# The order of a mixture-of-experts stage: small slots' weights behind the tile's, gates ahead of the routing's rest, tiles' experts behind the row list

## The chip, the cores and the metric

The kernel runs on one core of one Trainium2 chip. The metric is device time in microseconds (us) of one execution; three runs of the kernel before lie between 984.69 and 986.05 us, with a median of 985.2 us.

## The reference

Three stages in a row: attention with a memory term, a dense MLP on its output, and a mixture of experts (MoE), in which each of 2304 tokens goes to one of eight experts. The change touches the third stage alone.

```python
def _moe2_ref(x, w_gate, w_output_gate, w1, w2):
    logits = x @ w_gate
    e_idx = np.argmax(logits, axis=1)
    logits_s = logits - logits.max(-1, keepdims=True)
    probs = np.exp(logits_s)
    probs /= probs.sum(-1, keepdims=True) + 1e-09
    gate_w = probs[np.arange(N), e_idx]
    eom = 1.0 / (1.0 + np.exp(-(x @ w_output_gate)))
    for e in range(E):
        mask = e_idx == e
        h = np.maximum(x[mask] @ w1[e], 0.0)
        ye = h @ w2[e]
        out[mask] = gate_w[mask, None] * eom[mask, e, None] * ye
    return out

def reference(**kwargs):
    attn_out = _attn_ref(**attn_kwargs)
    x = np.ascontiguousarray(attn_out.transpose(0, 2, 1, 3)).reshape(B * S, H * D)
    x = _moe_ref(x=x, **moe_kwargs)
    return _moe2_ref(x=x, **moe2_kwargs)
```

N is 2304, D is 512, the hidden size F is 1024, and there are E = 8 experts. All data are float32.

## The kernel before

Attention and the MLP are interleaved and fill the first 700 us. The MLP's result is written to DRAM as `x2d`, one row per token, with four more columns for the gate factor. For the last block of tokens these columns are made late, by the generator `gates` (line 572): three small DVE operations, an Exp on ACT, three more DVE steps (line 578 on), and then the DMA of the rows to `x2d`.

The routing (`route`, line 820) counts tokens per expert and builds the order in which tokens are worked on. It is a generator; each `next(routing)` runs it to its next `yield`. It makes three lists. `idx` and `idxs` (line 914 on) name the token rows of each tile, from a one-hot product `inv` on TensorE (line 908) whose operand `rh` is made on DVE (lines 900 to 904). `ei` and `sw` (lines 901, 902) give each tile's expert, and whether it differs from that of the tile before; they come from the comparisons `c1` and `c2` (line 879 on). `idr`, `idq` and `esm` (lines 922 to 939) are rows and experts of the small slots, and need a second little product, `inq` (line 924), of `ivs` (line 922).

The experts' work is cut into tiles of 128 rows of one expert, numbered from 0. Tiles 0 and 1 belong to an expert picked early, from all but the last tokens; the routing's pieces are placed between their matmuls. The loop `tiles` (line 1078) does tiles 2 to 18, more if needed. In tile i, TensorE does the hidden layer (`hidden`, line 682: two halves of 512 columns, each in four steps of three matmuls, since each operand is split in a high and a low part), turns `hs`, the relu of the first half (`px`, line 667), and does the second layer (`result`, line 695, eight steps of three). Next to it ACT and DVE split the eight weight chunks of tile i+1, which lie in `st`, into `wH` (a cast, line 641) and `wL` (a subtraction, line 646); the same two engines split `hs` into `hH` and `hL` and the next rows into `xgH` and `xgL`. `Weights.fetch` (line 618) loads a chunk of 512 KB by a DMA from SP, under the condition that `sw` is not zero: a tile with the expert of the one before moves no data. A chunk's buffer comes free when its subtraction in the tile before is done.

Rows that do not fill a tile go into four small slots of 32 rows (`small`, line 1006), one beside each of the host tiles 4, 6, 9 and 11 (`HOSTS`). A slot's generator is started in the tile ahead of its host, where it reads its expert from `esm`, gathers its rows on POOL and loads its first four chunks (`sw`, line 1020). In the host it is moved on by `tick`, which `stepped` (line 1073) calls after each step of matmuls: turn of its rows and `xT`, product `ph` (line 1038) and the loads of its other four chunks (line 1022), relu `hq` (line 1043), turn `hT` (line 1049), nine empty steps, product `py` (line 1056), result `sy` (line 1060).

ACT, DVE, POOL and TensorE run the expert stage in the order in which the program is written. So do SP's DMAs, each behind the ones before it. The beginning of a tile reads, before the change:

```python
            if i + 1 in HOSTS and i + 1 < i1:
                ahead = small(HOSTS[i + 1])
                next(ahead)
            if i in HOSTS:
                beside = ahead
            more = i + 1 < i1
            w0, w = w, weights(i + 1) if more else None
            if i > i0:
                put(py, xlast, idxs[:, i - 1 : i])
            xnn = rows(idx[:, i + 2 : i + 3]) if i + 2 < i1 else None
            if more:
                w.fetch(0, 1, 2, 3, 4, 5, 7, 6)
```

Of the kernel before, what the change touches and what calls it, by code (L numbers as in the profile page):

```python
# [11 lines left out]
F32 = DT.float32  # L12
# [5 lines left out]
ALU = mybir.AluOpType  # L18
AX = mybir.AxisListType
# [3 lines left out]
P = 128  # L23
B, H, S, D = 4, 8, 576, 64
NT, DM, DFF = B * S, H * D, 2048
E, FF = 8, 1024
# [4 lines left out]
NS, SQ, SB = 4, 32, 4  # L31
NI = 24

NR = 19
HOSTS = {4: 0, 6: 1, 9: 2, 11: 3}
# [47 lines left out]
def tile_kernel(ctx, tc, qT, kT, qn, vx, z, beta, w_in, w_out, w_gates, w1, w2, out):  # L83
    nc = tc.nc
    PE, DVE, ACT, POOL, SP = nc.tensor, nc.vector, nc.scalar, nc.gpsimd, nc.sync
# [153 lines left out]
    c1 = at.enter_context(tc.tile_pool(name="c1", bufs=1, side="left"))  # L239
# [274 lines left out]
    part1, got = [], {}  # L514
# [98 lines left out]
    class Weights:  # L613
# [24 lines left out]
        def high(self, *cs):  # L638
            for c in cs:
                self.H[c] = self.pool.tile([P, 1024], F32R, name=f"wH{c}")  # L640
                ACT.copy(self.H[c], stage[c])  # L641
# [100 lines left out]
    def mid(x, n):  # L742

        return x.rearrange("p (o e) -> p o e", o=1).to_broadcast([P, n, x.shape[1]])

    def flat(x):
        return x.rearrange("p a b -> p (a b)")
# [72 lines left out]
    def route():  # L820
# [15 lines left out]
        DVE.tensor_copy(tt, tot)  # L836
        DVE.tensor_tensor(gtc, cnt.to_broadcast([P, E, NJ]), mid(io18, E), op=ALU.is_gt)
        yield
        DVE.tensor_tensor_scan(flat(inc), onef, flat(tt), 0.0, op0=ALU.mult, op1=ALU.add)
# [36 lines left out]
        DVE.tensor_copy(cf, ci)  # L876

        c1, c2 = (r2.tile([P, NI, E], F32, name=x) for x in ("c1", "c2"))
        DVE.tensor_tensor(c1, mid(flat(base), NI), itl.to_broadcast([P, NI, E]), op=ALU.is_le)
        DVE.tensor_copy(tf, ti)  # L880
        DVE.tensor_tensor(c2, mid(flat(end), NI), itl.to_broadcast([P, NI, E]), op=ALU.is_le)
        gates = got["gates"]
        next(gates)
        yield
        DVE.tensor_tensor(ohc[:, 0:6], mid(io128, 6), cf[:, 0:6].to_broadcast([P, 6, P]), op=ALU.is_equal)
        next(gates)
        DVE.tensor_tensor(c1, c1, c2, op=ALU.subtract)
        next(gates)
        DVE.tensor_tensor(ohc[:, 6:12], mid(io128, 6), cf[:, 6:12].to_broadcast([P, 6, P]), op=ALU.is_equal)
        next(gates)  # L890
        DVE.tensor_tensor(c1, c1, mid(io8, NI), op=ALU.mult)
        next(gates)
        yield
        DVE.tensor_tensor(ohc[:, 12:], mid(io128, NJ - 12), cf[:, 12:].to_broadcast([P, NJ - 12, P]), op=ALU.is_equal)
        yield
        ef = r2.tile([P, NI + 1, 1], F32, name="ef")
        DVE.memset(ef[:, 0:1], 0.0)
        DVE.tensor_reduce(ef[:, 1 : NI + 1], c1, axis=AX.X, op=ALU.add)
        rh = r2.tile([P, NJ, 3, NI + NS], BF16, name="rh")
        DVE.tensor_tensor(rh[:, :, 0], mid(ion, NJ), tf.to_broadcast([P, NJ, NI + NS]), op=ALU.is_equal)  # L900
        DVE.tensor_copy(ei, flat(ef)[:, 1 : NI + 1])
        DVE.tensor_tensor(sw, flat(ef)[:, 1 : NI + 1], flat(ef)[:, 0:NI], op=ALU.not_equal)
        DVE.tensor_scalar(rh[:, :, 1], rh[:, :, 0], iop, None, op0=ALU.mult)
# [10 lines left out]
        DVE.tensor_copy(idx, tok)  # L914

        DVE.tensor_scalar(iv[:, 0], iv[:, 0], -1.0e6, 1.0e6, op0=ALU.mult, op1=ALU.add)
        DVE.tensor_tensor(tok, tok, iv[:, 0], op=ALU.add)
# [3 lines left out]
        ivs = r.tile([P, 3, NS], BF16, name="ivs")  # L921
        DVE.tensor_copy(ivs, inv3[:, :, NI:])
        inq = ps_g.tile([P, 512], F32, name="inq", tag="pg")[:, : 3 * NS]
        PE.matmul(inq, lhsT=four, rhs=ivs.rearrange("p a n -> p (a n)"), start=True, stop=True)
# [8 lines left out]
        DVE.tensor_copy(idq, tks)  # L933
        c3 = r.tile([P, NS, E], F32, name="c3")
        DVE.tensor_tensor(c3, mid(flat(key), NS), ion[:, 1 : NS + 1].rearrange("p (n o) -> p n o", o=1).to_broadcast([P, NS, E]), op=ALU.is_equal)
        DVE.tensor_tensor(c3, c3, mid(io8, NS), op=ALU.mult)
        ef3 = r.tile([P, NS, 1], F32, name="ef3")
        DVE.tensor_reduce(ef3, c3, axis=AX.X, op=ALU.add)
        DVE.tensor_copy(esm, flat(ef3))
        yield  # L940
# [48 lines left out]
    def hidden_out():  # L989
        return hp_.tile([P, FF], F32, name="hs"), [hp_.tile([P, 8, P], F32R, name=f"h{x}") for x in "HL"]  # L990
# [15 lines left out]
    def small(s):  # L1006
# [32 lines left out]
        while len(ws) < 2 * KD:  # L1039
            fetch()  # L1040
        yield
        hq = smp.tile([P, FF // 4], F32, name="hq")
        ACT.activation(hq, ph, AF.Relu)
# [5 lines left out]
        ACT.copy(hT, pt.rearrange("p (c t) -> p c t", c=2))  # L1049
        for _ in range(9):  # L1050
            yield
# [19 lines left out]
    def stepped(g, n):  # L1071

        for _ in range(n):
            r_ = next(g)
            tick()
        return r_

    def tiles(i0, i1, w, xg, xn, xx):
        nonlocal beside, smp
        for i in range(i0, i1):  # L1080
            if i + 1 in HOSTS and i + 1 < i1:
                ahead = small(HOSTS[i + 1])
                next(ahead)
            if i in HOSTS:
# [6 lines left out]
            if more:  # L1091
                w.fetch(0, 1, 2, 3, 4, 5, 7, 6)
            high, low = (w.high, w.low) if more else (lambda *cs: None,) * 2

            hs, hh = hidden_out()
            tick()
# [10 lines left out]
            DVE.tensor_tensor(hh[1][:, 0:4], px, f32(hh[0][:, 0:4]), op=ALU.subtract)  # L1107
            ph = stepped(g, 2)
            high(3)
            relu(hs, ph, 1)  # L1110
# [31 lines left out]
    routing = route()  # L1142
# [77 lines left out]
```

## Time and profile before

| | us |
|---|---|
| median of the three runs | 985.2 |
| profiled execution, its own time | 991.04 |
| span of the profiled execution | 989.2 |
| TensorE (PE) busy | 917.4, 93% of the span |
| VectorE (DVE) busy | 622.1 |
| ScalarE (ACT) busy | 520.3 |
| GpSimd (POOL) busy | 367.7 |
| mean granted clock of TensorE | 0.973 |

Engine times are busy times in the one profiled execution, and L667 is line 667 of the kernel. In a row of the time line stand the start in us from the span's start, the duration in us, the engine, the line, the operation, its output <- its inputs, the shapes and the number of instructions that the row merges; in brackets, the idle time of the engine just before and what ended it. A row of busy time by stretches has the stretch, its length, then the busy us (and instructions) of PE, PEld (loads of the stationary operand), DVE, ACT and POOL, the granted clock as a share of 2.4 GHz, the share of time in which the DMA engines were busy, and GB/s. A row of waits says which instruction waited for which, us in total, how often, and the longest. In the page's groups of instructions the mean in ns of one follows the busy time.

### The profile page before, as it was taken

How to read it: one execution, taken by the hardware profiler on the slowest of the kernel's cores; microseconds unless marked ns; L12 is line 12 of the kernel's file. 1: busy time of each engine (PE TensorE's matmuls, PEld its weight loads, DVE VectorE, ACT ScalarE, POOL GpSimd, SP SyncE). 2: the span in 40 equal slices, each digit the busy share in tenths (PEclk: the TensorE clock that was granted, in tenths of full speed). 3: DMA queues.
4: the chain of work that ended last, by engine and by line, in shares of the span. 5: the costliest groups of instructions: out<-in, count | busy, mean ns of one | idle time of the engine just before them, and what ended most of it. 6: DMA issues, size and time to landing. Idle time of an engine off the chain costs nothing. (4 is left out here: it accounts for less than half of the span.)

```text
span 989.2 us, 17067 instructions
## 1 busy us (share of the span) xinstructions
PE 917.4 (93%) x5733; PEld 720.5 (73%) x5733; DVE 622.1 (63%) x1511; ACT 520.3 (53%) x1084; POOL 367.7 (37%) x574
## 2 busy tenths in 40 slices
PE   4677799999999999899999999999887999999996
PEld 2344477777776777788888888888766778778875
DVE  6766797565657541778344444447767668678982
ACT  5556666565546543445222222223346668768883
POOL 1543376445546552435533333335221123112210
PEclk9987799999999999989999999999999999999998
DMA  6432332221213010543011111112323565532850
GB/s 196 129 100 95 118 117 71 76 75 54 75 54 100 14 35 17 176 129 128 22 44 44 43 44 43 45 43 107 107 76 118 204 240 190 204 130 104 319 201 23
DMA packets 49278, 101.70 MB, mean 103 GB/s; under 512 B 5341, under 2 KB 15581, under 8 KB 49184
## 3 DMA queue, kind: packets, MB, share of 16 engines
q1 hardware_dynamic: 45696, 89.74, 26.8%
q0 software_dynamic: 3488, 10.80, 3.2%
q8 instruction: 47, 0.77, 0.3%
q14 instruction: 47, 0.39, 0.1%
HBM read 136.66 MB, written 14.72 MB: 153 GB/s over the span
## 5 line engine op out<-in xcount | busy, mean ns | idle before, releaser
L646 DVE TENSOR_TENSOR wL<-st,wH 128x1024 fp32r<-128x1024 f32 x136 | 163.7, 1227 | 43.2 <-ACT wH L641 37.5
L213 PE MATMUL hps<-xH,wH 128*128 128x256 f32 x576 | 166.8, 290 | 1.6 <-ACT xH L91 1.4
L213 PE MATMUL hps<-xL,wH 128*128 128x256 f32 x576 | 162.2, 282 | 2.9 <-DVE xL L200 2.9
L95 POOL TENSOR_SCALAR gH<-g 128x256 fp32r<-128x256 f32 x144 | 63.6, 441 | 271.8 <-DVE g L217 214.4
L365 POOL TENSOR_SCALAR a<-a,rs,omg 128x320 f32<-128x320 f32 (+4 forms) x160 | 126.9, 805 | 97.1 <-DVE rs L360 72.5
L213 PE MATMUL hps<-xH,wL 128*128 128x256 f32 x576 | 161.2, 280 | 0.0
L217 DVE SCALAR_TENSOR_TENSOR g<-g,hps 128x256 f32<-128x256 f32 x144 | 60.0, 417 | 146.4 <-ACT g L216 146.4
L641 ACT CAST wH<-st 128x1024 fp32r<-128x1024 f32 x136 | 139.7, 1053 | 8.5 <-DMA st<-w 8.4
L216 ACT ACTIVATE g<-hps,half 128x256 f32<-128x256 f32 x144 | 68.0, 472 | 137.4 <-PE hps L213 112.3
L213 PEld LDWEIGHTS hps<-xH,wH 128*128 128x128 f32 x576 | 108.9, 189 | 18.6 <-issue 12.6
L221 POOL TENSOR_TENSOR gL<-g,gH 128x256 fp32r<-128x256 f32 x144 | 115.4, 802 | 11.8
L213 PEld LDWEIGHTS hps<-xL,wH 128*128 128x128 f32 x576 | 109.1, 189 | 8.6 <-DVE xL L200 3.8
L352 ACT ACTIVATE a<-st,mn 64x64 f32<-64x64 f32 (+4 forms) x160 | 88.4, 555 | 48.0 <-DVE mn L343 48.0
L376 PE MATMUL pa<-ident,a 128*128 128x128 f32 (+1 forms) x480 | 81.9, 302 | 32.1 <-POOL a L365 28.5
L213 PEld LDWEIGHTS hps<-xH,wL 128*128 128x128 f32 x576 | 109.1, 190 | 0.1
L376 PEld LDWEIGHTS pa<-ident,a 128*128 128x128 f32 (+1 forms) x480 | 59.0, 151 | 60.6 <-POOL a L365 33.8
L182 PE MATMUL acc<-wH,gH 128*128 128x512 f32 x288 | 95.5, 413 | 1.3 <-POOL gH L95 1.2
L182 PE MATMUL acc<-wH,gL 128*128 128x512 f32 x288 | 91.7, 400 | 2.3 <-POOL gL L221 2.3
L337 PE MATMUL pa<-kd,qd 64*128 64x64 f32 (+5 forms) x384 | 83.7, 488 | 10.3 <-DVE mn L343 5.4
L182 PE MATMUL acc<-wL,gH 128*128 128x512 f32 x288 | 91.0, 397 | 0.0
L343 DVE CUSTOM_DVE_ANT_0 st<-pa,mask 64x64 f32<-64x64 f32 (+4 forms) x160 | 52.9, 372 | 33.0 <-PE pa L337 33.0
L182 PEld LDWEIGHTS acc<-wH,gL 128*128 128x128 f32 x288 | 54.2, 190 | 16.2 <-POOL gL L221 3.5
(239 smaller groups left out, 1674.6 us busy)
## 6 DMA issues: line engine op xcount, KB each, us to landing
st<-w SPq DMA_DIRECT2D x136, 512.0 KB
sw<-w SPq DMA_DIRECT2D x32, 512.0 KB
w<-w_in SPq DMA_DIRECT2D x16, 512.0 KB
w<-w_out SPq DMA_DIRECT2D x16, 512.0 KB
qnt<-qn SPq DMA_DIRECT2D x16, 320.0 KB
vt<-vx SPq DMA_DIRECT2D x16, 320.0 KB
x2d<-row SPq DMA_DIRECT2D x18, 258.0 KB
qd<-qT SPq DMA_DIRECT2D x16, 288.0 KB
```

The lines of the kernel that those rows point to most:

```text
L95: POOL.tensor_scalar(out, x, 1.0, 1.0, op0=ALU.mult, op1=ALU.mult)
L182: PE.matmul(acc[t], lhsT=gg[:, t * P : (t + 1) * P], rhs=ww[:, 512:1024], start=m == 0 and first, stop=m == HM - 1 and last)
L213: PE.matmul(hps, lhsT=ww[:, kk * P : (kk + 1) * P], rhs=xx[:, kk], start=k == 0, stop=k == 3 * KD - 1)
L216: ACT.activation(g, hps, AF.Relu, bias=half, scale=1.0 / 6.0)
L217: DVE.scalar_tensor_tensor(g, g, 1.0, hps, op0=ALU.min, op1=ALU.mult)
L221: ENG[GL].tensor_tensor(gL, g, f32(gH), op=ALU.subtract)
L337: PE.matmul(pss[j][: QN[i], o : o + k1 - k0], lhsT=self.qd[r, QS[i] : QS[i] + QN[i]], rhs=self.kd[r, k0:k1], start=True, stop=True)
L352: ACT.activation(self.a[j][:m, o + D : o + D + n], self.st[j][i][:m, :n], AF.Exp, bias=self.mn[j][:m, i : i + 1], scale=-1.0, accum_out=se ...
L365: ENG[NORM[i]].tensor_scalar(av, av, r[:m, i], omg[:m, h : h + 1], op0=ALU.mult, op1=ALU.mult)
L376: PE.transpose(psa[:, off : off + QN[i]], self.a[j][: QN[i], QO[i] + c * P : QO[i] + (c + 1) * P], ident[: QN[i], : QN[i]])
L641: ACT.copy(self.H[c], stage[c])
L646: DVE.tensor_tensor(self.L[c], stage[c], f32(self.H[c]), op=ALU.subtract)
```

## The change

Four things are moved; no operation is added or left out.

1. In `route`, the first step of `gates` is run three segments earlier, right after `gtc`; the other four steps stay beside the one-hot `ohc`.
2. `c1`, `c2`, `ef`, `ei` and `sw` are computed after `idx`, no longer before `rh`.
3. `esm` is computed ahead of the product `inq`, with a `yield` between them, and both pieces run inside tile 2: one at its start, one after the hidden layer. Before, they ran after tile 2.
4. In `tiles`, a small slot is started behind the tile's own `put`, `rows` and `fetch`; in `small`, four empty steps stand before `hq`, and six in place of nine before `py`.

```diff
@@ route
         DVE.tensor_tensor(gtc, cnt.to_broadcast([P, E, NJ]), mid(io18, E), op=ALU.is_gt)
+        gates = got["gates"]
+        next(gates)
         yield
...
         DVE.tensor_copy(cf, ci)
-
-        c1, c2 = (r2.tile([P, NI, E], F32, name=x) for x in ("c1", "c2"))
-        DVE.tensor_tensor(c1, mid(flat(base), NI), itl.to_broadcast([P, NI, E]), op=ALU.is_le)
         DVE.tensor_copy(tf, ti)
-        DVE.tensor_tensor(c2, mid(flat(end), NI), itl.to_broadcast([P, NI, E]), op=ALU.is_le)
-        gates = got["gates"]
-        next(gates)
         yield
         DVE.tensor_tensor(ohc[:, 0:6], mid(io128, 6), cf[:, 0:6].to_broadcast([P, 6, P]), op=ALU.is_equal)
         next(gates)
-        DVE.tensor_tensor(c1, c1, c2, op=ALU.subtract)
         next(gates)
         DVE.tensor_tensor(ohc[:, 6:12], mid(io128, 6), cf[:, 6:12].to_broadcast([P, 6, P]), op=ALU.is_equal)
         next(gates)
-        DVE.tensor_tensor(c1, c1, mid(io8, NI), op=ALU.mult)
         next(gates)
         yield
...
-        ef = r2.tile([P, NI + 1, 1], F32, name="ef")
-        DVE.memset(ef[:, 0:1], 0.0)
-        DVE.tensor_reduce(ef[:, 1 : NI + 1], c1, axis=AX.X, op=ALU.add)
         rh = r2.tile([P, NJ, 3, NI + NS], BF16, name="rh")
         DVE.tensor_tensor(rh[:, :, 0], mid(ion, NJ), tf.to_broadcast([P, NJ, NI + NS]), op=ALU.is_equal)
-        DVE.tensor_copy(ei, flat(ef)[:, 1 : NI + 1])
-        DVE.tensor_tensor(sw, flat(ef)[:, 1 : NI + 1], flat(ef)[:, 0:NI], op=ALU.not_equal)
...
         DVE.tensor_copy(idx, tok)
+        c1, c2 = (r2.tile([P, NI, E], F32, name=x) for x in ("c1", "c2"))
...
+        DVE.tensor_copy(ei, flat(ef)[:, 1 : NI + 1])
+        DVE.tensor_tensor(sw, flat(ef)[:, 1 : NI + 1], flat(ef)[:, 0:NI], op=ALU.not_equal)
...
         DVE.tensor_copy(ivs, inv3[:, :, NI:])
+        c3 = r.tile([P, NS, E], F32, name="c3")
...
+        DVE.tensor_copy(esm, flat(ef3))
+        yield
         inq = ps_g.tile([P, 512], F32, name="inq", tag="pg")[:, : 3 * NS]
...
         DVE.tensor_copy(idq, tks)
-        c3 = r.tile([P, NS, E], F32, name="c3")
...
-        DVE.tensor_copy(esm, flat(ef3))
         yield
@@ small
         yield
+        for _ in range(4):
+            yield
         hq = smp.tile([P, FF // 4], F32, name="hq")
...
-        for _ in range(9):
+        for _ in range(6):
             yield
@@ tiles
-            if i + 1 in HOSTS and i + 1 < i1:
-                ahead = small(HOSTS[i + 1])
-                next(ahead)
             if i in HOSTS:
                 beside = ahead
...
                 w.fetch(0, 1, 2, 3, 4, 5, 7, 6)
+            if i + 1 in HOSTS and i + 1 < i1:
+                ahead = small(HOSTS[i + 1])
+                next(ahead)
             high, low = (w.high, w.low) if more else (lambda *cs: None,) * 2
+            if i == 2:
+                next(routing)
             hs, hh = hidden_out()
...
             ph = stepped(g, 2)
+            if i == 2:
+                next(routing)
             high(3)
```

On ACT, in the routing beside tile 0's second layer, the order was (`t` is the gate's Exp of the logits, `so` the gate step's own Exp, `hH` the cast of the turned `hs`, `ys` the result of tile 0):

```order
L564 ACTIVATE t_7987<-t_7986 128x16
L671 CAST hH<-px 128x512
L576 ACTIVATE so<-so 128x2
L707 ACTIVATE ys<-py,xg 128x512
L693 ACTIVATE hs<-ph 128x512
```

and it is now

```order
L564 ACTIVATE t_7987<-t_7986 128x16
L576 ACTIVATE so<-so 128x2
L671 CAST hH<-px 128x512
L707 ACTIVATE ys<-py,xg 128x512
L693 ACTIVATE hs<-ph 128x512
```

The Exp of `so` now stands ahead of the cast of `hH`.

On SP, in tile 3, the first small slot's loads (`sw`, L1020, with the read of `esm` before them) stood ahead of the tile's own (`st`, L636). The brackets name what each waits for:

```order
L1009 TENSOR_LOAD esm [waits DVE_49]
...
L1020 DMA sw<-w 128x1024 [waits DVE_49,PE_49,DMAHW0_49,Activation_49,Pool_49]
...
L1020 DMA sw<-w 128x1024 [waits DMAHW1_49]
...
L1020 DMA sw<-w 128x1024 [waits DMAHW2_49]
...
L1020 DMA sw<-w 128x1024 [waits DMAHW3_49]
...
L636 DMA st<-w 128x1024 [waits DMAHW4_49,Activation_49]
...
L636 DMA st<-w 128x1024 [waits DMAHW5_49,Activation_49]
```

They now stand behind the last of the tile's eight:

```order
L636 DMA st<-w 128x2x512 [waits DMAHW5_49,DVE_49]
...
L636 DMA st<-w 128x2x512 [waits DMAHW6_49,DVE_49]
...
L636 DMA st<-w 128x2x512 [waits DMAHW7_49,DVE_49]
...
L1010 TENSOR_LOAD esm [waits DVE_49]
...
L1021 DMA sw<-w 128x1024 [waits DMAHW0_49,PE_49,Pool_49]
...
L1021 DMA sw<-w 128x1024 [waits DMAHW1_49]
```

The tile's eight have moved in front of the read of `esm`, and each now waits for a subtraction on DVE (DVE_49).

On ACT, in tile 4, a host tile, the small slot's `hq` and `hT` stood ahead of the casts of the first two weight chunks and the relu of `hs`:

```order
L1033 COPY xT<-px 128x128
L1043 ACTIVATE hq<-ph 128x256
L1049 COPY hT<-pt 128x256
L641 CAST wH_8784<-st 128x1024
L641 CAST wH_8786<-st 128x1024
L693 ACTIVATE hs<-ph 128x512
L641 CAST wH_8793<-st 128x1024
L1105 CAST hH<-px 128x512
L641 CAST wH_8817<-st 128x1024
L693 ACTIVATE hs<-ph 128x512
```

They now stand behind that relu, one on each side of the cast of `hH`:

```order
L1034 COPY xT<-px 128x128
L641 CAST wH_8777<-st 128x1024
L641 CAST wH_8779<-st 128x1024
L693 ACTIVATE hs<-ph 128x512
L641 CAST wH_8786<-st 128x1024
L1046 ACTIVATE hq<-ph 128x256
L1110 CAST hH<-px 128x512
L1052 COPY hT<-pt 128x256
L641 CAST wH_8817<-st 128x1024
L693 ACTIVATE hs<-ph 128x512
```

Between the two relus of `hs` ACT has two more operations than before.

## Rows read from the trace of the kernel before

**Rows 1.** Busy time by stretches, tile 3 and tile 5.
```profile
748.90:767.20 18.30, 14.38 (x61) 11.19 (x60) 11.91 (x21) 10.41 (x13) 3.07 (x3) 0.91 0.45 159
786.00:798.70 12.70, 12.70 (x61) 9.95 (x60) 11.73 (x12) 11.32 (x15) 4.66 (x3) 1.00 0.39 144
```

**Rows 2.** TensorE's waits, 711 to 768 us.
```profile
PE px L667 <- ACT hs L693: 4.8, 2, 3.9
PE inv L908 <- DVE rh L904: 1.4, 1, 1.4
PE inq L924 <- DVE ivs L922: 1.3, 1, 1.3
```

**Rows 3.** TensorE's waits, 768 us to the end.
```profile
PE px L667 <- ACT hs L693: 3.0, 4, 0.8
PE py L701 <- DVE hL L1107: 1.1, 4, 0.3
```

**Rows 4.** Time line of TensorE in tile 3.
```profile
757.25 0.66 PE L667 MATMUL px<-ident,hs 128*128 128x128 f32 x4 [3.92 <-ACT hs L693]
...
758.34 0.63 PE L688 MATMUL ph<-wH,xgL 128*128 128x512 f32 x1
...
761.86 0.39 PE L701 MATMUL py<-wH,hL 128*128 128x512 f32 x1
```

**Rows 5.** Time line of ACT in tile 3.
```profile
754.71 1.99 ACT L641 CAST wH<-st 128x1024 fp32r<-128x1024 f32 x2 [6.42 <-DMA st<-w]
```

**Rows 6.** Time line of SP's DMA issues in tile 3.
```profile
752.04 2.13 SPq L1020 DMA_DIRECT2D sw<-w  x4
754.62 13.96 SPq L636 DMA_DIRECT2D st<-w  x16
```

**Rows 7.** Time line of DVE at the start of tile 3.
```profile
749.08 0.17 DVE L926 COPY iq<-inq 128x12 f32<-128x12 f32 x1 [0.26 <-PE inq L924]
...
750.22 0.17 DVE L933 CAST idq<-tks 128x4 uint32<-128x4 f32 x1
...
750.96 0.17 DVE L939 CAST esm<-ef 128x4 int32<-128x4 f32 x1
```

**Rows 8.** Time line of ACT in the routing.
```profile
711.61 0.59 ACT L671 CAST hH<-px 128x512 fp32r<-128x512 f32 x1 [1.07 <-PE px L667]
720.22 0.20 ACT L576 ACTIVATE so<-so 128x2 f32<-128x2 f32 x1 [8.02 <-DVE so L575]
```

**Rows 9.** Time line of DVE in the routing.
```profile
712.94 0.68 DVE L672 TENSOR_TENSOR hL<-px,hH 128x512 fp32r<-128x512 f32 x1
...
719.54 0.35 DVE L881 TENSOR_TENSOR c<-end,itl 128x192 f32<-128x192 f32 x1
719.81 0.17 DVE L573 TENSOR_TENSOR t<-oh,lg 128x16 f32<-128x16 f32 x1
...
720.10 0.95 DVE L885 TENSOR_TENSOR ohc<-io,cf 128x768 bf16<-128x768 f32 x1
...
725.48 0.68 DVE L904 TENSOR_TENSOR rh<-rh,io 128x504 bf16<-128x504 bf16 x1
```

**Rows 10.** Time line of TensorE in the routing.
```profile
713.52 0.40 PE L701 MATMUL py<-wH,hH 128*128 128x512 f32 x1
```

**Rows 11.** Time line of ACT in tile 4, a host tile.
```profile
767.95 0.26 ACT L1033 COPY xT<-px 128x128 f32<-128x128 f32 x1
771.28 0.39 ACT L1043 ACTIVATE hq<-ph 128x256 f32<-128x256 f32 x1 [3.08 <-PE ph L1038]
772.30 0.37 ACT L1049 COPY hT<-pt 128x256 f32<-128x256 f32 x1 [0.64 <-PE pt L1047]
```

**Rows 12.** Busy time by stretches, 724 to 732 us.
```profile
724.00:732.00 8.00, 6.34 (x37) 5.08 (x37) 3.89 (x15) 0.81 (x2) 2.04 (x2) 0.79 0.46 134
```

**Rows 13.** The page's groups of instructions: a weight subtraction on DVE.
```profile
L646 DVE TENSOR_TENSOR wL<-st,wH 128x1024 fp32r<-128x1024 f32 x136 | 163.7, 1227 | 43.2 <-ACT wH L641 37.5
```

**Rows 14.** Busy time by stretches, the small slot's first load.
```profile
752.00:762.40 10.40, 6.48 (x25) 4.93 (x24) 5.87 (x6) 6.40 (x8) 2.96 (x3) 0.84 0.79 278
```

More of the change, by code (lines that the diff above doesn't have):

```diff
@@ L914, in route @@
         DVE.tensor_copy(idx, tok)
+        c1, c2 = (r2.tile([P, NI, E], F32, name=x) for x in ("c1", "c2"))
+        DVE.tensor_tensor(c1, mid(flat(base), NI), itl.to_broadcast([P, NI, E]), op=ALU.is_le)
+        DVE.tensor_tensor(c2, mid(flat(end), NI), itl.to_broadcast([P, NI, E]), op=ALU.is_le)
+        DVE.tensor_tensor(c1, c1, c2, op=ALU.subtract)
+        DVE.tensor_tensor(c1, c1, mid(io8, NI), op=ALU.mult)
+        ef = r2.tile([P, NI + 1, 1], F32, name="ef")
+        DVE.memset(ef[:, 0:1], 0.0)
+        DVE.tensor_reduce(ef[:, 1 : NI + 1], c1, axis=AX.X, op=ALU.add)
+        DVE.tensor_copy(ei, flat(ef)[:, 1 : NI + 1])
+        DVE.tensor_tensor(sw, flat(ef)[:, 1 : NI + 1], flat(ef)[:, 0:NI], op=ALU.not_equal)
         DVE.tensor_scalar(iv[:, 0], iv[:, 0], -1.0e6, 1.0e6, op0=ALU.mult, op1=ALU.add)
@@ L922, in route @@
         DVE.tensor_copy(ivs, inv3[:, :, NI:])
+        c3 = r.tile([P, NS, E], F32, name="c3")
+        DVE.tensor_tensor(c3, mid(flat(key), NS), ion[:, 1 : NS + 1].rearrange("p (n o) -> p n o", o=1).to_broadcast([P, NS, E]), op=ALU.is_equal)
+        DVE.tensor_tensor(c3, c3, mid(io8, NS), op=ALU.mult)
+        ef3 = r.tile([P, NS, 1], F32, name="ef3")
+        DVE.tensor_reduce(ef3, c3, axis=AX.X, op=ALU.add)
+        DVE.tensor_copy(esm, flat(ef3))
+        yield
         inq = ps_g.tile([P, 512], F32, name="inq", tag="pg")[:, : 3 * NS]
@@ L933, in route @@
         DVE.tensor_copy(idq, tks)
-        c3 = r.tile([P, NS, E], F32, name="c3")
[L935 to L938, printed above, removed]
-        DVE.tensor_copy(esm, flat(ef3))
         yield
```

## Prediction

> **What bounds the kernel now.** I read the busy time by stretches first, then TensorE's waits, then the time lines of the engines around the waits that are left. An ordinary tile of the expert stage, tile 5, takes 12.70 us, all of them busy on TensorE; ACT is busy for 11.32 and DVE for 11.73 of them [rows 1]. So TensorE sets the time there, and the other two have 1.0 to 1.4 us to spare. Tile 3 does the same work in 18.30 us, with 14.38 us of TensorE and a granted clock of 0.91 [rows 1]. From the routing to the end of tile 3 TensorE waits in three places that the change touches: 4.8 us for hs in two waits (the longest 3.9), 1.4 us for rh, 1.3 us for ivs [rows 2]. Behind it, one wait of 0.8 for hs and one of 0.3 for hL come back in each of the four host tiles, 3.0 and 1.1 us in all [rows 3]. No more than some 13 us are to be had from these waits and the slow clock that follows them.
>
> The wait of 3.92 us in tile 3 ends with the relu of hs [rows 4]. That relu stands on ACT behind two casts of weights, which begin at 754.71 after 6.42 us of waiting for a DMA of st [rows 5]. Those DMAs begin only at 754.62, because SP first issues the four DMAs of small slot 0 (752.04), and these need esm, which DVE writes last of all, at 750.96 [rows 6, 7]. The casts begin 0.09 us after the first st is issued, so this DMA moved nothing: tile 4 has tile 3's expert. SP held up work that needed no data.
>
> **A. Routing.** The change sets three DVE operations and an Exp on ACT ahead of the split of px, and takes c1, c2 and their followers out from before the row list.
>
> The loss first. In the new order ACT has the Exp ahead of the cast hH, which before began at 711.61 [rows 8]. The three operations cost DVE 0.29 us (719.81 to 720.10 [rows 9]). They begin where hL stood, at 712.94, so the Exp begins near 713.35, the cast (0.59) ends near 714.05, and hL begins 1.15 us later than before. DVE is served in order, so the whole routing chain behind hL is late by 1.15. TensorE wants hH at 713.52 [rows 10]: it stands for about 0.6, and 0.3 more for hL.
>
> Then the gain. The three operations leave their old place (0.29). Five operations of c1's kind (0.27 each by c2's 719.54 to 719.81 [rows 9]) and two small casts (about 0.1 each) leave too: 1.8 in all. They had also filled gaps between dependent operations; three such gaps open again, 0.1 to 0.15 each, so 1.4 remain. rh, whose last operation begins at 725.48 [rows 9], is ready 1.4 - 1.15, some 0.3 us earlier. TensorE waits for rh anyway (1.4 [rows 2]), so its new wait for hH is paid from that wait. The 0.9 us for hs that is the second wait in the 4.8 [rows 2] goes as well: it came from the old place of the Exp, at 720.22 on ACT ahead of the relu [rows 8]; but it too only moves into the wait for rh. **A is 0.3 us**; bounds -0.9 (DVE wins nothing back) and +1.4 (the cast is not held up). ei and sw come some 4 us later; tile 3's weights are issued later by that, under the hidden layer of tile 2, at no cost as long as they need no data.
>
> **B. Tile 2.** The wait of 1.3 us for ivs [rows 2] goes, since ivs is made at the tile's start, where DVE waits for casts. In return the chain from iq to idq, 749.08 to 750.39, 1.3 us [rows 7], stands between two weight subtractions in mid tile and delays the second hL. DVE has 1.0 us free in a tile [rows 1], so I let 0.35 us reach TensorE, and 0.05 for the matmul. **B is 0.9**, between 0 (all of the chain shows) and 1.3.
>
> **C. Tile 3.** esm is written in tile 2; the st DMAs of tile 3 are ahead of the small slot's. The casts find their data, the relu is in time. Tile 3 becomes like tile 5: 18.3 - 12.7 = **5.6 us** [rows 1]. The check: 3.92 of waiting, and then matmuls that take 0.63 in place of the usual 0.39 or so, some eight at about 0.2 us more from start to start [rows 4]. Bounds 4.5 and 5.6.
>
> **D. Host tiles.** Before, ACT does xT, then waits 3.08 us for the small product before hq, and 0.64 more for the turn before hT; only then come the two casts and the first relu of hs [rows 11]. Now xT is followed by casts and relu at once. Of the 3.0 + 1.1 us [rows 3] all goes, unless it comes back later in the tile: hq (0.39), hT (0.37) and the wait for the turn (up to 0.64) [rows 11] now stand between the two relus of hs, 1.4 us against the 1.4 us that ACT has free [rows 1]. What is late next is the second relu. I leave 0.2 us in each tile: **D is 3.3 us**, between 0 and 4.1.
>
> The last move, small slots' first weights behind the tile's, with their gather behind the tile's scatter and gather on POOL, I cost at nothing: a whole tile of 12.7 us covers it. What it costs without that cover is the last rival.
>
> The sum is 0.3 + 0.9 + 5.6 + 3.3 = 10.1 us. The profiled execution, 991.04 us (its span 989.2), would come to 980.9. It lies 5.8 above the median of the runs, 985.2; taking the same sum from that gives **975.1 us**.
>
> **Rivals.**
> *The clock stays up too.* From 724 to 732 the granted clock was 0.79 [rows 12]: TensorE at the lower level for some 3.4 of 8 us, a loss of 1.7. If the shorter stops leave it high, 973.4 us. Against it: A only moves the stops, it hardly shortens them.
> *The host tiles' waits move, and do not go.* ACT has no time over in these tiles, so the second relu takes the first one's place: D is 0, 978.4 us.
> *The Exp holds the routing up.* A is -0.9 and B 0: 977.2 us. For it: the cast behind a DVE result, on an engine that serves in order; against it: the 1.8 us taken out.
> *The change does not do what it says in tile 3.* The st DMAs now wait for tile 2's subtractions, which the iq chain pushes back. If the casts still wait as long, C is 0: 980.7 us. Against it: st 0 comes free after the first subtraction, most of a tile earlier.
> *Gains are swallowed*, by several of these together: within 0.2%.
> *Slower: the small slots' operands come late.* Their first four DMAs are issued behind the tile's eight, which wait for the subtractions that end the tile before, two of them at 1.23 us [rows 13]: up to 2.5 us into the tile ahead of the host. The host's small product cannot begin before xT is done, at 768.21 in a tile that begins at 767.2 [rows 11, 1]: 12.7 - 2.5 + 1.0 = 11.2 us from issue to need. Last time it took 10.4 us, at 278 GB/s, 2.9 MB with the gathers of that time [rows 14]. So it holds by a narrow margin, with the first chunk due first. It turns to a loss where the load takes over 14 us in all four hosts; at 16 us, 975.1 + 4 x 4.8 = 994 us. The Trainium skill, "DMA: Bandwidth & Descriptors", section "Queues, rings and completion order", says that a DMA engine takes one issuer's descriptors in ring order; both kinds of weights come from SP. By that rule a tile's eight chunks with data (4.2 MB) ahead of the small slot's would double the load, at that rate to some 23 us, and every host would lose about 11 us. The trace speaks against that here: those 2.9 MB hold four small chunks (2.1 MB) and no others, though st DMAs were issued from 754.62 on [rows 14, 6].
>
> **How the numbers follow.** Forecast 0.55, clock 0.15, host waits 0.12, Exp 0.07, tile 3 unmended 0.03, swallowed 0.03, late operands 0.05. The range takes in forecast, clock, host waits and Exp, with the bounds of A to D: **971.5 to 979.0 us**. A difference of 0.2% (2 us) is about what a measurement of this kernel can tell from none. Faster than that: 0.92; within it 0.03; slower 0.05.
>
> **What would show it.** Right: in tile 3 no wait of TensorE for hs and a clock of 1.00; the wait for ivs gone; in the host tiles less than 0.3 us for hs and hL together; a new wait of about 0.6 us for hH next to 714 us, and rh ready at most half a microsecond earlier than before. Wrong: a wait of TensorE for the small slots' weights or rows at the start of tiles 4, 6, 9 and 11; a tile 3 above 13.5 us; host tiles as long as before; a second relu of hs that TensorE waits for by more than half a microsecond.

## The result and the profile after

The changed kernel takes 975.77 us (median of four runs, 974.74 to 978.34), the kernel before 985.62 on the same chip (four runs, 984.69 to 986.71): a ratio of 0.9903, with an interval of 0.9881 to 0.9926. It is 9.85 us faster; 10.1 were predicted. The profiled execution took 974.74 us with a span of 973.0, against 991.04 and 989.2.

Of the 16.2 us between the two spans, 3.69 lie ahead of the first product of the routing, `pf` (711.96 and 708.27 us), where both kernels run the same instructions, so these belong to the executions and not to the change. From there on, TensorE's waits in the changed kernel, from 705 us on (what waited for which, us in total, times, the longest):

```profile
PE py L701 <- DVE hL L672: 1.5, 2, 0.8
PE inv L897 <- DVE rh L893: 1.1, 1, 1.1
PE pf L760 <- DVE ohb L822: 0.4, 1, 0.4
PE py L701 <- ACT hH L671: 0.4, 1, 0.4
```

The 4.8 and 1.3 us of [rows 2] and the 3.0 and 1.1 us of [rows 3] are gone. All that is left lies in the routing; from 728 us to the end the profile lists no wait of TensorE. The busy time by stretches of the changed kernel, tile 3 and then tile 5 (the columns of [rows 1]):

```profile
743.56:756.24 12.68, 12.68 (x61) 9.94 (x59) 11.63 (x12) 11.10 (x14) 3.53 (x3) 1.00 0.61 230
773.69:786.37 12.68, 12.68 (x61) 9.94 (x60) 11.74 (x12) 11.30 (x15) 3.11 (x3) 1.00 0.68 232
```

Tile 3 is now as long as tile 5, without an idle moment and at the full clock, where it took 18.30 us at 0.91 [rows 1]. The time line of SP's DMA issues beside it:

```profile
727.50 17.68 SPq L636 DMA_DIRECT2D st<-w  x16
746.04 2.06 SPq L1021 DMA_DIRECT2D sw<-w  x4
```

SP has issued the tile's last `st` (by 745.18) before it comes to the four loads of the small slot. These have 11.4 us up to the small product at 757.49, which waits for none of them; 11.2 were worked out in the prediction. ACT in host tile 4:

```profile
756.94 0.26 ACT L1034 COPY xT<-px 128x128 f32<-128x128 f32 x1
757.08 2.01 ACT L641 CAST wH<-st 128x1024 fp32r<-128x1024 f32 x2
761.82 0.60 ACT L693 ACTIVATE hs<-ph 128x512 f32<-128x512 f32 x1 [2.72 <-PE ph L688]
762.31 1.04 ACT L641 CAST wH<-st 128x1024 fp32r<-128x1024 f32 x1
763.25 0.39 ACT L1046 ACTIVATE hq<-ph 128x256 f32<-128x256 f32 x1
763.59 0.59 ACT L1110 CAST hH<-px 128x512 fp32r<-128x512 f32 x1
764.49 0.37 ACT L1052 COPY hT<-pt 128x256 f32<-128x256 f32 x1 [0.32 <-PE pt L1050]
764.76 1.05 ACT L641 CAST wH<-st 128x1024 fp32r<-128x1024 f32 x1
765.72 0.60 ACT L693 ACTIVATE hs<-ph 128x512 f32<-128x512 f32 x1
```

In the 3.08 us in which ACT stood for the small product [rows 11] it now does the two casts, and the first relu waits only for its own product. The second relu (765.72, done at 766.32) is ready 0.06 us before TensorE turns it at 766.38. In the other three host tiles these are 0.06 or 0.07 us, in ordinary tiles some 0.7: the room between the two relus is used up, and one more operation there would show.

The routing is the one place with new waits. In the changed kernel ACT and DVE read there, DVE first:

```profile
709.45 0.17 DVE L575 TENSOR_REDUCE so<-t 128x2 f32<-128x16 f32 x1
710.36 0.69 DVE L672 TENSOR_TENSOR hL<-px,hH 128x512 fp32r<-128x512 f32 x1 [0.74 <-ACT hH L671]
...
721.67 0.68 DVE L893 TENSOR_TENSOR rh<-rh,io 128x504 bf16<-128x504 bf16 x1
...
723.86 0.35 DVE L906 TENSOR_TENSOR c<-base,itl 128x192 f32<-128x192 f32 x1
...
726.34 0.34 DVE L918 CAST idxs<-tok 128x24 uint32<-128x24 f32 x1
726.43 0.68 DVE L672 TENSOR_TENSOR hL<-px,hH 128x512 fp32r<-128x512 f32 x1
```

```profile
709.65 0.20 ACT L576 ACTIVATE so<-so 128x2 f32<-128x2 f32 x1 [2.81 <-DVE so L575]
709.76 0.57 ACT L671 CAST hH<-px 128x512 fp32r<-128x512 f32 x1
```

The cast `hH` waits for the Exp, DVE stands 0.74 us for the cast, and the whole chain follows late, as foreseen. What was not foreseen is the last line of DVE above: the chain from `c1` to `sw` now stands between the row list and the next `hL`. TensorE's time line has the waits there; the last is the one for that `hL`, while the 0.65 us ahead of `inv` go on into the wait for `rh`, which TensorE has anyway:

```profile
710.38 0.50 PE L701 MATMUL py<-wH,hH 128*128 128x512 f32 x1 [0.38 <-ACT hH L671]
720.83 0.50 PE L701 MATMUL py<-wH,hL 128*128 128x512 f32 x1 [0.65 <-DVE hL L672]
722.40 0.85 PE L897 MATMUL inv<-rh,ohc 128*128 128x84 bf16 x18 [1.07 <-DVE rh L893]
727.17 0.50 PE L701 MATMUL py<-wH,hL 128*128 128x512 f32 x1 [0.83 <-DVE hL L672]
```

### The profile page after: what moved, and what is told of

It is laid out like the page before. It is cut to its first block, busy times and chain, and to the rows that moved or that the text cites. A ratio compares the mean times of both kernels' runs of the same rounds, so it can differ in the third digit from the quotient of the medians.

```text
span 973.0 us, 17079 instructions
## 1 busy us (share of the span) xinstructions
PE 910.9 (94%) x5733; PEld 715.8 (74%) x5733; DVE 623.0 (64%) x1511; ACT 520.5 (53%) x1084; POOL 367.8 (38%) x574
## 5 line engine op out<-in xcount | busy, mean ns | idle before, releaser
L708 POOL DMA_INDIRECT out<-ys,idxs x17 | 18.8, 1107 | 132.4 <-ACT ys L707 84.1
```

## The experiments

Twelve runs were made, of ten more kernels, of the changed kernel once more (after2) and of one of the ten once more (v1b), each beside the kernel before on the same chip. "To list" is the time from the start of `pf` to the start of `inv`, "to tile 2" that from `inv` to the turn of the rows of tile 2, each in the profiled execution. The four of the first group change the kernel before; the others change the changed kernel.

| kernel | median | ratio to before, interval | to list | to tile 2 |
|---|---|---|---|---|
| before (profile above) | 985.62 | | 14.25 | 6.96 |
| changed | 975.77 | 0.9903, 0.9881 to 0.9926 | 14.13 | 6.51 |
| e_hq | 981.83 | 0.9941, 0.9919 to 0.9964 | 14.23 | 6.97 |
| e_order | 981.01 | 0.9942, 0.9919 to 0.9965 | 14.23 | 5.40 |
| e_esm | 979.63 | 0.9941, 0.9918 to 0.9965 | 14.22 | 5.40 |
| e_tiles | 980.36 | 0.9937, 0.9916 to 0.9958 | 14.21 | 5.41 |
| e_noroute | 975.72 | 0.9879, 0.9858 to 0.9900 | 14.24 | 5.40 |
| u_gates | 975.82 | 0.9881, 0.9852 to 0.9909 | 13.11 | 6.50 |
| u_experts | 977.44 | 0.9916, 0.9884 to 0.9948 | 16.14 | 6.98 |
| v1 | 977.58 | 0.9894, 0.9861 to 0.9926 | 13.21 | 6.97 |
| after2 | 976.79 | 0.9890, 0.9849 to 0.9931 | 14.12 | 6.50 |
| v1b | 972.96 | 0.9851, 0.9815 to 0.9887 | 13.22 | 5.41 |
| x_behind | 998.67 | 1.0106, 1.0075 to 1.0137 | 14.13 | 6.50 |
| x_ahead | 1010.79 | 1.0199, 1.0142 to 1.0256 | 14.11 | 6.96 |

### One part of the change alone, on the kernel before

**e_hq**: only the later relu and turn in the host tiles.

```diff
         yield
+        for _ in range(4):
+            yield
         hq = smp.tile([P, FF // 4], F32, name="hq")
...
-        for _ in range(9):
+        for _ in range(6):
```

> The kernel before with one part of the change: in a host tile the small slot's relu hq and turn hT stand four steps later (and six empty steps in place of nine before its second product). Theory: the two casts of weights and the first relu of hs no longer stand behind hq and hT on ACT, so the wait of TensorE for hs goes in each of four host tiles, and nothing comes back later in the tile. Measured from start to start of matmuls that is 1.36 us a tile (18.80 us before, 17.45 in the whole change), 5.4 us in all: about 980 us. Rival 1, the sizing of the prediction (waits of 0.76 + 0.28 less 0.2 left over): 3.3 us, about 982.3 us. Rival 2, the second relu of hs becomes the new wait: no change, 985.5 us, and a wait of TensorE for hs at the second turn.

From the start of one small slot's turn (`px` from `sx`, L1031) to that of the next, tiles 4 and 5 take 30.13 us instead of 31.48. The changed kernel has the same 30.13; the two rows are from the kernel before and from the changed one:

```profile
767.25:798.73 31.48, 30.45 (x223) 23.07 (x222) 22.78 (x23) 23.21 (x32) 7.86 (x6) 1.00 0.49 178
756.24:786.37 30.13, 30.13 (x223) 23.12 (x223) 22.68 (x23) 23.26 (x32) 6.81 (x6) 1.00 0.54 185
```

That is 1.35 less for this host. In the changed kernel the other three give 1.31, 1.36 and 1.32 (the last up to the turn of the last tile's rows), 5.34 in all. TensorE's waits in e_hq from 705 us on:

```profile
PE px L667 <- ACT hs L693: 4.8, 2, 3.9
...
PE inq L924 <- DVE ivs L922: 1.3, 1, 1.3
```

The host tiles' waits for `hs` and `hL` are gone, and those of the routing and of tiles 2 and 3 are left. Nothing that the profile lists comes back later in the tile: the part is worth some 5.3 us. The times say 5.8, by the interval 3.6 to 8.0, and so leave the 3.3 of the smaller sizing just outside.

**e_order**: only the start of the small slots behind the tile's own DMAs.

```diff
-            if i + 1 in HOSTS and i + 1 < i1:
-                ahead = small(HOSTS[i + 1])
-                next(ahead)
...
                 w.fetch(0, 1, 2, 3, 4, 5, 7, 6)
+            if i + 1 in HOSTS and i + 1 < i1:
+                ahead = small(HOSTS[i + 1])
+                next(ahead)
```

> The kernel before with one part of the change: a small slot is started behind the tile's own put, rows and fetch; esm is still made after tile 2. Theory (the place in SP's queue decides): in tile 3 the st DMAs no longer stand behind the read of esm, the casts are in time, and tile 3 shrinks from 18.3 to 12.7 us; the wait of 1.3 us for ivs stays: about 980 us. The small slot's load then begins near 752 us and needs up to 10 us; its product comes near 763, so a wait there is possible, up to 2 us. Rival (it is the late esm that holds the tile up, wherever its reader stands): tile 3 stays at about 18 us, 985.5 us.

**e_esm**: only `esm` ahead of `inq`, and both inside tile 2.

```diff
         DVE.tensor_copy(ivs, inv3[:, :, NI:])
+        c3 = r.tile([P, NS, E], F32, name="c3")
...
+        DVE.tensor_copy(esm, flat(ef3))
+        yield
         inq = ps_g.tile([P, 512], F32, name="inq", tag="pg")[:, : 3 * NS]
...
+            if i == 2:
+                next(routing)
             hs, hh = hidden_out()
```

> The kernel before with one part of the change: esm and the small slots' rows are made inside tile 2; the small slot's loads still stand ahead of the tile's on SP. Theory: the reader of esm finds it written, so the st DMAs behind it are issued before the casts of tile 3 want them; tile 3 shrinks to 12.7 us and the wait of 1.3 us for ivs goes: 5.7 + 1.1 = 6.8 us less, about 979 us; then either of the two parts alone would have mended tile 3. Rival (the loads' place in the queue matters in itself): the four small DMAs ahead wait for something else, free space or an earlier load, and tile 3 keeps 2 us or more of its wait: 981 to 984 us.

The wait of 3.9 us is gone in either of them; the five for `hs` that are left (the four host tiles' and the routing's) are 0.8 us at most. From e_order and then from e_esm, TensorE's waits from 705 us on:

```profile
PE px L667 <- ACT hs L693: 3.8, 5, 0.8
...
PE inq L924 <- DVE ivs L922: 1.3, 1, 1.3
```

```profile
PE px L667 <- ACT hs L693: 3.9, 5, 0.8
...
PE py L701 <- DVE hL L1110: 1.1, 4, 0.3
```

So the loss in tile 3 needed both: `esm` late, and SP behind it. Either half mends it, and neither rival came (no gain for e_order, 2 us or more of the wait left for e_esm). e_order keeps the wait for `ivs` and takes on one of 0.2 us for the gather of the slot's rows, so by the waits the earlier `esm` is the better half; the times (0.9942 and 0.9941) do not tell the two apart. The chain was the predicted one, SP, then `st`, then the casts, then the relu.

**e_tiles**: both together.

```diff
+        DVE.tensor_copy(esm, flat(ef3))
+        yield
...
                 w.fetch(0, 1, 2, 3, 4, 5, 7, 6)
+            if i + 1 in HOSTS and i + 1 < i1:
+                ahead = small(HOSTS[i + 1])
+                next(ahead)
```

> The kernel before with both parts that concern tiles 2 and 3 (esm inside tile 2, small slots started behind the tile's fetch), without the later hq and without the moves of gates and experts. Theory: tile 2 gains 1.1 us and tile 3 5.7 us, the host tiles stay at 18.8 us: about 979 us. Together with the run that moves hq alone the gains should add up to those of the whole change less 0.1 to 0.6 us for the routing. Rival (the parts need each other): the host tiles get longer, since the loads come later while hq stands early; more than 980.5 us.

It is not measurably better than e_esm alone (the intervals lie over each other), as the two mend the same loss. Its 0.63% and the 0.59% of e_hq add up to 1.22%; the next kernel, which joins them, has 1.21%. Within the intervals, some 0.2% each, the terms do not eat each other.

### The routing

**e_noroute**: the changed kernel with the routing's moves undone.

```diff
-        gates = got["gates"]
-        next(gates)
         yield
...
+        c1, c2 = (r2.tile([P, NI, E], F32, name=x) for x in ("c1", "c2"))
...
         DVE.tensor_copy(tf, ti)
+        DVE.tensor_tensor(c2, mid(flat(end), NI), itl.to_broadcast([P, NI, E]), op=ALU.is_le)
+        gates = got["gates"]
+        next(gates)
```

> The whole change without its two moves in the routing: gates and the tiles' experts stay where they were before. The stretch from the product pf to the turn of tile 2's rows is measured in the profile; it took 20.64 us in the change, 21.21 in the kernel before with the granted clock down at its end, and 19.62 in three variants with the old routing and the clock up. Theory: the two moves lose 1.0 us when the clock stays up (a new wait of 0.8 us for hL behind the experts' chain), so this kernel does the stretch in 19.6 us (21.2 with the clock down) and is 1 us or more faster than the change where the clock is up: about 974.8 us. Rival (the moves gain 0.3 us, as the prediction had it): 976 us, and a stretch of 20.9 us.

**u_gates**: only the gates' first step back in its old place. Between the old place and the new one lies a single `yield` of `route`, so the step was moved by one segment, and not by three as point 1 of the change has it.

```diff
-        gates = got["gates"]
-        next(gates)
...
         DVE.tensor_copy(tf, ti)
+        gates = got["gates"]
+        next(gates)
```

> The whole change, but the first step of gates back in its old place behind the list's positions; the experts' chain stays behind the row list. Theory: the Exp no longer stands ahead of the cast hH, so the wait for hH (0.4 us) goes and DVE's chain is 1.2 us earlier; rh is ready 1.2 us earlier than in the kernel before, though the wait of 0.9 for hs comes back; the wait of 0.8 for hL behind the experts' chain stays. The stretch from pf to tile 2's rows takes about 19.5 us against 20.64, so 974.7 us. Rival (the Exp's place costs nothing, since TensorE waits for rh anyway): the stretch stays at 20.6 us.

Their two stretches, `pf` to `inv` and `inv` to tile 2, from e_noroute, u_gates and the changed kernel:

```profile
711.83:726.07 14.24, 11.74 (x52) 8.86 (x52) 13.62 (x61) 2.69 (x6) 1.45 (x1) 1.00 0.15 56
726.07:731.47 5.40, 5.40 (x41) 4.49 (x40) 1.73 (x7) 0.59 (x1) 2.04 (x2) 1.00 0.28 73
```

```profile
710.58:723.69 13.11, 11.74 (x52) 8.86 (x52) 12.38 (x53) 2.69 (x6) 1.31 (x1) 1.00 0.16 60
723.69:730.19 6.50, 5.65 (x40) 4.41 (x40) 3.55 (x15) 0.59 (x1) 2.16 (x2) 1.00 0.30 84
```

```profile
708.27:722.40 14.13, 12.03 (x52) 8.78 (x51) 12.64 (x53) 3.15 (x6) 1.11 (x1) 1.00 0.15 56
722.40:728.91 6.51, 5.68 (x41) 4.41 (x41) 3.56 (x15) 0.59 (x1) 2.17 (x2) 1.00 0.31 84
```

All six stretches are at the full clock, so the moves can be priced apart. From the first pair to the second only the experts' chain goes: eight DVE instructions leave the stretch ahead of `inv` (61 to 53) and eight come to the one behind it (7 to 15). It gives 1.13 us and takes 1.10. From the second pair to the third the gates' step goes ahead: it takes 1.02 us and gives nothing. At the full clock the routing's moves lose 1.0 us in all (19.64 to 20.64). The medians cannot tell an effect of 0.1%: e_noroute's ratio is 0.24% lower than the changed kernel's, with intervals that overlap.

At the lower clock the loss does not show. The stretch from `inv` to tile 2, from the kernel before and then from x_ahead (below), which has the changed kernel's routing:

```profile
726.21:733.17 6.96, 6.96 (x40) 5.69 (x40) 1.73 (x7) 0.59 (x1) 2.04 (x2) 0.75 0.32 79
728.42:735.38 6.96, 6.96 (x40) 5.71 (x40) 3.55 (x15) 0.58 (x1) 2.17 (x2) 0.75 0.41 118
```

Both take 6.96 us, and x_ahead has no wait for that `hL`: TensorE is slow enough for DVE to be in time. The loss of 1.0 us belongs to the executions in which the clock stays up there.

**u_experts**: only the chain back, in one block ahead of `rh`.

```diff
+        c1, c2 = (r2.tile([P, NI, E], F32, name=x) for x in ("c1", "c2"))
...
+        DVE.tensor_tensor(sw, flat(ef)[:, 1 : NI + 1], flat(ef)[:, 0:NI], op=ALU.not_equal)
         rh = r2.tile([P, NJ, 3, NI + NS], BF16, name="rh")
```

> The whole change, but the tiles' experts (c1 to sw) computed ahead of rh again; the first step of gates stays early. Theory: rh is 1.3 us later than in the change and TensorE waits for it by so much more, but the wait of 0.8 us for hL behind the list goes; the stretch from pf to tile 2's rows is about 20.5 to 20.9 us against 20.64: no difference, 975.8 us. Rival (the experts' chain costs nothing behind the list, since TensorE has other work there): the stretch grows by the whole 1.3 us, to 21.9 us.

TensorE's wait for `rh` there:

```profile
PE inv L907 <- DVE rh L903: 3.1, 1, 3.1
```

The block costs 16.14 - 14.13 = 2.0 us ahead of `inv`, where 1.3 were expected, and then `inv` to tile 2 is at a clock of 0.76. The two stretches come to 23.12 us, above both the theory (20.5 to 20.9) and the rival (21.9); how much of the 6.98 behind `inv` is the clock's, this run cannot say. In the old order the same operations were strewn between others and cost 1.13. In one block the operations that need the one before begin 0.39 us after it, where two of the same size that do not (`c1` and `c2`) are 0.26 apart; strewn between others they fill such gaps. This is what the prediction argued when it kept 1.4 of 1.8 us; what came is 0.12 + 1.11 = 1.2.

**v1**: the changed kernel with the gates' first step behind `hL`, and the chain a segment later, behind the split that it held up.

```diff
+        yield
         gates = got["gates"]
         next(gates)
-        yield
...
+        DVE.tensor_copy(idxs, tok)
+        yield
         c1, c2 = (r2.tile([P, NI, E], F32, name=x) for x in ("c1", "c2"))
...
     split4(px, hh, 4)
+    next(routing)
```

> The whole change with both moves in the routing mended: the first step of gates one segment later, behind the subtraction hL, so that the Exp stands behind the cast hH; and the experts' chain one segment later, behind the next split of hs. Theory: no wait for hH, none for hL behind the list, rh 0.9 us earlier than in the change: the stretch from pf to tile 2's rows takes 18.7 us against 20.64, and the kernel 974 us. Rival (the stretch is bound by the chain of DVE whatever stands where): 19.6 us or more, and no gain over the variant without the two moves.

**after2** and **v1b** are the changed kernel and v1 once more, side by side.

> The changed kernel once more, with a second profile. Theory: the stretch from the product pf to the turn of tile 2's rows takes 20.6 us again where the granted clock stays up behind the list's product, and some 22 us where it falls; the stretch ahead of the routing, from the turn of xg to pf, 13.0 or 14.6 us by the same (both seen in other runs of the same instructions). The time is 975 to 978 us. Rival: a stretch outside these two pairs, so that something else than the clock varies.

> The variant with both routing moves mended once more, beside the change on the same chip. Theory: list's product 13.2 us behind pf, then 5.4 us to the turn of tile 2's rows with the clock up (18.6 in all, 2.0 less than the change), or 7.0 with the clock down (20.2); about 1 to 2 us faster than the change. Rival (what the clock takes back is as large as the gain): no difference to the change.

The stretch behind `inv` of after2, then both stretches of v1b, then the one behind `inv` of v1:

```profile
720.98:727.48 6.50, 5.67 (x40) 4.42 (x40) 3.55 (x15) 0.59 (x1) 2.16 (x2) 1.00 0.31 83
```

```profile
707.09:720.31 13.22, 11.50 (x52) 8.94 (x51) 12.48 (x53) 2.91 (x6) 1.11 (x1) 1.00 0.16 60
720.31:725.72 5.41, 5.41 (x41) 4.44 (x40) 3.60 (x15) 0.59 (x1) 2.03 (x2) 1.00 0.30 73
```

```profile
724.67:731.64 6.97, 6.97 (x41) 5.86 (x41) 3.61 (x15) 0.59 (x1) 2.04 (x2) 0.76 0.29 78
```

At one clock v1b's routing is 18.63 us, 2.0 shorter than the changed kernel's and 1.0 shorter than the old one's. TensorE's wait for `hH` and the one for the `hL` behind the list are gone in it; the 0.65 us for the `hL` ahead of `inv` stay. Its median is 3.8 us below that of after2, measured beside it, with intervals of the ratios that overlap (0.9849 to 0.9887); in the runs of v1, whose profile has the lower clock behind `inv`, it was no better than u_gates measured beside it. That v1 is the fastest of these kernels is shown for the routing at the full clock, and not shown for the whole.

### Small slots' loads with all weights moved

In the changed kernel the tiles ahead of hosts have no weights of their own to load: tiles 3 and 5 move 230 and 232 GB/s (rows above), some 2.9 MB, of which the four small chunks are 2.1 and POOL's gathers and scatter the rest; tiles 8 and 10 move 214 and 231. So the order of loads cannot show there. Here every tile's weights are loaded, whether its expert is new or not; no result depends on that. **x_behind** is the changed kernel with this, and **x_ahead** has the small slots' loads ahead of the tile's in addition.

```diff
-        return Weights(i, er, SP.value_load(sw[0:1, i : i + 1], min_val=0, max_val=1))
+        return Weights(i, er)
```

```diff
+            if i + 1 in HOSTS and i + 1 < i1:
+                ahead = small(HOSTS[i + 1])
+                next(ahead)
...
                 w.fetch(0, 1, 2, 3, 4, 5, 7, 6)
-            if i + 1 in HOSTS and i + 1 < i1:
-                ahead = small(HOSTS[i + 1])
-                next(ahead)
```

> The changed kernel, but every tile's weights are loaded, also where the expert stays the same, so that the eight chunks ahead of the small slot's always carry 4.2 MB. Theory (the queue is served in order): the small slots' loads now stand behind real data; TensorE waits for the small product in the host tiles; together with the DMA traffic that nearly fills the 250 us of the stage (some 97 MB) the kernel gets 10 to 25 us slower than the change. Rival (a whole tile of cover is enough even so): no wait for the small slots' weights, and under 5 us more than the change.

> The same with every tile's weights loaded, but the small slots' first loads ahead of the tile's again, as in the kernel before. Theory: the wait moves from the small product to the casts of the tile's weights, and so to TensorE's wait for hs; the same traffic bounds it, so the time is within 5 us of the run with the loads behind. Rival (the order ahead is the better one where data move): over 5 us faster than that run.

TensorE's waits in the expert stage, x_behind first and x_ahead second:

```profile
PE py L1059 <- DMA sw<-w: 8.4, 11, 1.4
PE px L1032 <- DMA sx<-x2d,idr: 3.4, 2, 2.5
PE ph L1039 <- DMA sw<-w: 1.3, 2, 0.6
PE px L667 <- ACT hs L693: 0.5, 1, 0.5
```

```profile
PE px L667 <- ACT hs L693: 19.0, 4, 6.3
PE py L1059 <- DMA sw<-w: 2.3, 4, 0.7
```

The loads issued behind are the ones that come late in the main: the small slots' in x_behind, the tile's (by way of the casts and the relu) in x_ahead, where 2.3 us for small chunks are left. That agrees with the rule from the Trainium skill, "DMA: Bandwidth & Descriptors", section "Queues, rings and completion order", that a DMA engine takes one issuer's descriptors in ring order. The price differs: a late small chunk stops TensorE for 1.4 us at most, a late tile chunk for up to 6.3. Busy time of a stretch of x_behind from tile 4 on:

```profile
757.80:792.02 34.22, 28.74 (x207) 19.99 (x207) 19.67 (x20) 21.34 (x30) 7.25 (x6) 1.00 1.04 398
```

The DMA engines are full there (a share of 1.04, 398 GB/s), and both orders leave TensorE waiting. x_behind's median is 21.9 us above that of after2, within the 10 to 25 expected. Between the two orders the expectation failed: not within 5 us of each other, and the order ahead is not the better one. By the medians the changed order is 12 us better, by the ratios 9. The spans differ by 11.7, but 4.75 of that lie ahead of `pf` (709.56 and 714.31 us), where both run the same instructions; from `pf` on it is 7.0 us.

## Why the prediction was right

**The whole.** 975.1 was forecast and 975.77 came, with the range and the direction right. The sum of 10.1 against 9.85 is closer than its terms: A was put too high and D too low. The measurement could not have told 10.1 from 11 (interval 7.3 to 11.7 us).

**A, routing: 0.3 forecast, a loss of 1.0 at equal clock.** Up to `inv` the working holds. `hL` begins 2.09 us after `pf` instead of 0.98, 1.11 later where 1.15 was said; TensorE's wait for `hH` is 0.38 where 0.6 was said; `rh` is ready 0.12 us earlier instead of 0.3. The step that failed is "at no cost": the prediction had `ei` and `sw` come later for free, and only looked at who needs them. It did not look at what stands behind them on DVE, the next `hL`. TensorE waits 0.83 us for that and loses 1.10, which eats the 1.13 won ahead of `inv`; what remains is the 1.02 that the gates' step costs. In the pair of profiles above, the old stretch ran at 0.75 and took 6.96 us, so A seems to win 0.57 there (21.21 to 20.64); u_gates and e_noroute show that this is the clock, and at the full clock the moves are a loss. At the lower clock on both sides A is 21.21 to 21.07 (x_ahead), a gain of 0.14.

**B, tile 2: 0.9 forecast, 1.07 measured** (14.45 to 13.38 us, from its first hidden product to that of tile 3, before and after):

```profile
734.45:748.90 14.45, 13.14 (x62) 10.07 (x62) 12.12 (x13) 11.92 (x15) 2.70 (x2) 1.00 0.11 38
730.18:743.56 13.38, 13.26 (x62) 10.04 (x62) 12.13 (x23) 11.23 (x14) 2.72 (x2) 1.00 0.12 41
```

The wait for `ivs` is gone. The second `hL` does come late: its first product begins 0.51 us after the one before it, where 0.23 is usual, so the delay cost about 0.3, where 0.35 was said.

**C, tile 3: 5.6 forecast, 5.67 measured** (18.35 to 12.68 us). e_order and e_esm show the cause.

**D, host tiles: 3.3 forecast, 5.3 measured**, 1.31 to 1.36 in each. The mechanism held; two sizes failed. The 1.4 us that ACT has free were read from tile 5, which hosts no slot. The term of 0.2 us for a late second relu was too much: it comes in time, if only by 0.06 us, since `hq`, `hT` and the wait for the turn took 0.39 + 0.37 + 0.32 = 1.1 us and not 1.4. And the prediction took the idle time of [rows 3] (0.76 and 0.28, 1.04 in a tile) for the whole loss. Matmul records overlap, about 0.39 us long at 0.23 us from start to start, so a wait also takes the overlap: in host tile 4 of the kernel before, the two products that waited begin 1.15 and 0.67 us after the ones before them, which is 0.92 and 0.44 over the usual 0.23, 0.16 more than each idle time.

**The sum again.** Measured within the profiled pair, A to D are 0.57 + 1.07 + 5.67 + 5.34 = 12.65 us, and with the 3.69 ahead of `pf` 16.3, against 16.2 between the spans. With A at the full clock on both sides it is 11.1. The medians show 9.85, by the interval of the ratio 7.3 to 11.7; after2's 0.989 is 10.8. That the forecast lay so near is partly luck: A and D missed in opposite directions.

**The rivals.** The clock staying up (973.4) happens in some profiles with the old routing (e_order) and with the new (after2), and stays down in others with either, so nothing here shows it to be the change's doing. The host waits did not move. The Exp did hold the routing up, by 1.0 us. So the rival's end for A (-0.9) was right in size, though DVE did win 1.13 us back and lost it again behind the list; B, which the rival set to 0, was not. Tile 3 is mended, and the gains were not swallowed. The small slots' operands were not late, since no tile ahead of a host had data of its own to load. Where all have, x_behind shows late operands, as the rival said, but a smaller price than its 11 us for each host (23 less 11.2 is nearer 12): 21.9 us in all by the medians, other late loads included; and the order of before would have lost more.

## What to carry to other kernels

SP's issues stood behind a read of `esm` until 752.04 us, and with them, until 754.62, a DMA that moved no data and the casts that waited 6.42 us for it [rows 5, 6]. When an engine waits for a DMA, look at what stands ahead of it on the issuing engine, and put what is ready ahead of what is not. When a chain is moved to a place where its result is not yet needed, price it by what stands behind it on its own engine. A wait between overlapping matmuls cost more than its idle time, here 0.16 us each, so take its price from start to start.

## What was not expected of the hardware

Behind `inv` the same 41 matmuls of the old order take 5.40 us at a granted clock of 1.00 in e_noroute, and 6.96 at 0.75 in the kernel before (the 1.2 GHz level for part of it). Both have the same wait of 1.4 us for `rh` in front. v1 and v1b, one kernel, differ in the same way (6.97 at 0.76, 5.41 at 1.00). So one wait does not decide the level, and two profiles of one kernel can differ by 1.6 us in a stretch of 5; the clock was read beside every stretch compared here. The stretch ahead of the routing differs too: `pf`, up to which all these kernels run the same instructions, begins anywhere from 706.45 (e_order) to 714.31 us (x_ahead), so profiles are compared here from `pf` on. What decides the level was not settled.
